# Ten of twelve normalised tiles of the second MoE turned by DMA in 16-bit words in place of TensorE

## The chip, the cores and the metric

The kernel runs on one core of one Trainium2 chip. The metric is the device time of one execution in microseconds; a kernel's figure is the median of several executions. The engines are named as in the profile: PE is TensorE (matmuls and, with an identity matrix as operand, transposes), ACT is ScalarE, DVE is VectorE, POOL is GpSimd, and SP is SyncE, which issues the DMAs here.

## The reference

The program is a chain of three blocks. All results are float32, to float32's accuracy.

```
attn = masked attention: q, k, v of 2 batches x 8 heads x 768 tokens x 64; a key counts for a query when
       the 6 sign bits of q @ proj and k @ proj agree; softmax; times v
x  = attn as 1536 tokens x 512
# first MoE
h  = x @ w_in (512 x 2048);  g = h * tanh(softplus(h));  x = g @ w_out (2048 x 512)
# second MoE
h  = x @ w_in (512 x 1024);  sm = softmax(h);  solu = h * sm
ln = (solu - mean(solu)) / sqrt(var(solu) + 1e-6) * g_ln
out = ln @ w_out (1024 x 512)
```

The change concerns the last line: `ln` comes out of the normalisation with tokens on partitions, and the product with `w_out` wants the 1024 features on partitions, so every tile of 128 tokens x 1024 features has to be turned.

## The kernel before

A matmul in float32 accuracy is made of three matmuls in the shorter type FP32R: each operand is split into a high part (ACT, a copy that rounds) and a low part (DVE or POOL, the difference), and high times high, high times low and low times high are summed in PSUM.

The second MoE goes over the 1536 tokens in 12 tiles of 128. Its steps have these names in the planner and these lines in the profile:

- `sy` (L918 on ACT, L920 on DVE): the split of the tile's 512 input features into high and low.
- `u2` (L927, L928, L931): 24 matmuls of 128x512 into two PSUM banks, the tile's `h`.
- `n2` (L939 to L966): the softmax and the normalisation as a chain of 14 steps between DVE and ACT. Step 0 is the row maximum of `h` (L939, DVE), step 1 the exponential into the SBUF tile `e` (L941, ACT), step 4 `e` times `h` (L947, DVE; the last reader of `h`), step 6 the squares (L952, ACT), steps 7 and 8 the inverse root (L954, L956, ACT), steps 9 to 12 its refinement on 128x1 columns (L958 to L964, DVE), step 13 the normalised tile, again in `e` (L966, DVE).
- `t2` (L974): eight 128x128 float32 transposes on PE into two PSUM banks.
- `l2` (L980 on ACT, L983 on DVE): the high and low part of each half (512 columns) of the turned tile, `lh` and `ll`.
- `d2` (L991, L992, L993): 2 x 12 matmuls of 128x512 with `w_out`.
- `ot` (L997, ACT) copies the result out of PSUM and `od` (L1002) stores it with a DMA from SP's queue.

Each engine has one instruction stream that it works off in order. That order is written by a planner, `program_order` and `Order.run`: every step is an operation with its engine, a cost, a due time and the buffers that it reads and writes; a list-scheduling pass picks, engine by engine, what is ready first, and the instructions are then recorded in exactly that order. Buffers are rings: an operation that opens a new buffer waits until the last reader of the one `n` places before has finished. For the second MoE `h2=2` (two pairs of banks for `h`), `t2=1`, `e2=3` (three tiles `e`), `lh=3` (three pairs `lh`/`ll`), `ot=2`. The numbers are given twice, in the dictionary `rings` for the planner and as `bufs` of the tile pools.

In the attention block some score tiles are already turned by DMA: `tdma` (L1254) issues `dma_start_transpose` from SP on the high and low float16 parts of a tile, 128 x 1536 two-byte values, that is 12 blocks of 128 x 128. That step's input is made by ACT (L1229) and POOL (L1251).

Of the kernel before, what the change touches and what calls it, by code (L numbers as in the profile page):

```python
# [9 lines left out]
F32 = mybir.dt.float32  # L10
F32R = mybir.dt.float32r
F16 = mybir.dt.float16
I32 = mybir.dt.int32
AF = mybir.ActivationFunctionType
ALU = mybir.AluOpType
# [18 lines left out]
    load=19.06, vload=18.96, split0=-188.88, rest0=28.62, split1=-216.02, rest1=37.27, turn=-44.19,  # L34
# [22 lines left out]
    up=0.7, a0=0.494, a1=0.335, a2=0.602, a3=0.613, a4=0.52, a9=0.52, a10=1.25, da=0.464, db=0.2265,  # L57
    sy0=0.52, sy1=0.602, u2=1.39, n0=1.131, n1=1.091, n2=0.069, n3=0.075, n4=1.196, n5=0.069, n6=1.133,
    n7=0.188, n8=0.094, n9=0.069, n10=0.13, n11=0.069, n12=0.069, n13=0.723, t2=0.87, d2=2.72,
)  # L60
WIRE = dict(load=1.3, load0=0.65, vload=1.3, wload=1.65, copy=1.08, bdma=0.2, tdma=1.6,
            od=0.728, const0=0.185, const1=0.028, const2=0.028, const3=0.448)
LATENCY = dict(
    PE=dict(PE=0.0, Activation=0.2, DVE=0.2, Pool=0.2, SP=0.1),
# [10 lines left out]
class Order:  # L75
# [38 lines left out]
    def shared(self, o):  # L114

        key, engine = o[0], o[1]
        if engine == "Pool":
            return True
        if engine != "DVE":
            return False  # L120
        k = key[0]
        if k in ("hi", "sy"):
            return True
        if k == "first":
            return True
        if k == "w":
            return key[2] == 6
        if k == "n2":
            return key[3 - 1] == 13
        return False  # L130
# [5 lines left out]
    def run(self):  # L136
        ops, n = self.ops, len(self.ops)
# [13 lines left out]
        free = dict(BEGIN)  # L151
# [49 lines left out]
        for _ in range(n):  # L201
            best = None
            for e, line in queue.items():
                cand = []
                for r, i in line:
                    r = max(r, free[e])
                    if ops[i][7]:
                        r = ring(i, r)[0]
                        if r is None:
                            continue  # L210
                    cand.append((r, due[i], i))
                if not cand:
                    continue
                first = min(cand)[0]
                pick = min((c for c in cand if c[0] <= first + self.slack), key=lambda c: c[1:])
                if best is None or pick[0] < best[0]:
                    best = (pick[0], e, pick[2])
            at, e, i = best
            o = ops[i]
            queue[e] = [x for x in queue[e] if x[1] != i]  # L220
            for tok, name, m, k in ring(i, at)[1]:
                place[tok] = k
                held[name][k:k + m] = [tok] * m
            for tok in o[7]:
                if tok[0] in taken:
                    taken[tok[0]].append(tok)
            start[i] = at
            if o[8] is not None:
                hw = max(at + 0.05, hw) + o[2]
                begin = max(hw + 0.65, wire)  # L230
                wire = done[i] = begin + o[8]
                if e == "SP":
                    free[e] = begin + 0.85 if o[0][0] == "tdma" else hw
                else:
                    free[e] = at + 0.05
            else:
                if shared[i]:
                    at = start[i] = max(at, port[other[e]])
                    port[e] = at + o[2]
                free[e] = done[i] = at + o[2] * (2 if e == "PE" and at < COLD and o[0][0] != "warm" else 1)  # L240
            got.append(i)
            for tok in o[10]:
                busy[tok] -= 1
                was = idle.setdefault(tok, {})
                was[frm[i]] = max(was.get(frm[i], 0.0), done[i])
            for j in then[i]:
                left[j] -= 1
                if not left[j]:
                    queue[ops[j][1]].append((ready(j), j))
# [17 lines left out]


def program_order(pairs, tiles, routes, evac, chunks, wide, due, rings, stores, slack, queues=(), pooled=0,
                  gates=(0, 0, 0, 0), early=8, attention_only=False, split="G", again="AA", soon=0):  # L270

    order = Order(rings, stores, slack, due)
    op = order.op
    span = 2 * tiles
    lead = -2.0 * span
    A, V, G, T = "Activation", "DVE", "Pool", "PE"
# [255 lines left out]
    for t in range(12):  # L532
        at = N0 + t * TN
        b = 2 - t // 4
        ys = ("yp",) if t == 0 else ("xs", 0, (t - 1) % 4)
        yn = [("yn", b, o) for o in range(4)]
        for g in range(2 if b == 1 else 1):
            n = 2 if b == 1 else 1
            op(("sy", t, g, 0), A, COST["sy0"] / n, at, "sy0", yn, [ys])
            op(("sy", t, g, 1), V, COST["sy1"] / n, at, "sy1", yn, [ys])  # L540
        for kk in range(4):
            behind = [("mi", 47, 2), ("w", 47, 4)] if t == kk == 0 else []
            op(("u2", t, kk), T, COST["u2"], at, "u2", [ys, ("ws", 8 + 2 * kk), ("ws", 9 + 2 * kk)], [("h2", t)], 0,
               behind)
        h, e, s = ("h2", t), ("e2", t), ("s2", t)
        chain = [(V, [h, ("room", 3)], [s]), (A, [h, s], [e, s]), (V, [s], [s]), (V, [s], [s]), (V, [h, s, e], [e, s]),
                 (V, [s], [s]), (A, [e, s], [("j2", t), s]), (A, [s], [s]), (A, [s], [s]), (V, [s], [s]), (V, [s], [s]),
                 (V, [s], [s]), (V, [s], [s]), (V, [e, s], [e])]
        for i, (en, r, w) in enumerate(chain):
            op(("n2", t, i), en, COST["n%d" % i], at, "n%d" % i, r, w)  # L550
        op(("t2", t), T, COST["t2"], at, "t2", [e], [("t2", t)])
        for a in range(2):
            op(("l2", t, a, 0), A, COST["x1"], at, "l0", [("t2", t)], [("lh", t, a)])
            op(("l2", t, a, 1), V, COST["x2"], at, "l1", [("t2", t)], [("lh", t, a)])
        for a in range(2):
            op(("d2", t, a), T, COST["d2"], at, "d2",
               [("lh", t, a)] + [("xs", 2 - a, k) for k in range(4)], [("o2", t)])
        op(("ot", t), A, COST["x1"], at, "ot", [("o2", t)], [("ot", t)])
        dma(("od", t), at, "od", [("ot", t)])
# [19 lines left out]
def lsh_attention_moe_kernel(  # L579
# [17 lines left out]
    ab=2,  # L597
    nb=3,
    gb=2,
    cb=1,  # L600
    lnb=3,
    eb=8,
    p16b=6,
    ptb=8,
# [1 line left out]
    early=5,  # L606
# [3 lines left out]
    gates=(0, 0, 0, 0),  # L610
# [4 lines left out]
    split="G",  # L615
    again="VV",
    soon=4,
):
    nc = tc.nc
    B, H, S, D = q.shape  # L620
# [7 lines left out]
    DF2 = w2_in.shape[1]  # L628
# [62 lines left out]
    pools, parts, raw_w = {}, {}, {}  # L691
# [86 lines left out]
    def two_banks(*tok):  # L778
        return banks[:, order.place[tok]:order.place[tok] + 2]
# [6 lines left out]
    def step(name, make):  # L786

        def run(*key):
            if key[-1] == 0:
                gen[name, key[:-1]] = make(*key[:-1])  # L790
            next(gen[name, key[:-1]])
        return run
# [108 lines left out]
    ysp, ln_t, lt_t, out_t = ({} for _ in range(4))  # L901
# [31 lines left out]
    def norm2(t):  # L933
        h = two_banks("h2", t).rearrange("p a n -> p (a n)")
        s = pools["st2"].tile([128, 16], F32, tag="s", name="s")
        col = lambda i: s[:, i:i + 1]
        e = pools["tm2"].tile([128, DF2], F32, tag="e", name="e", bufs=3)
        ln_t[t] = e
        nc.vector.reduce_max(col(0), h, axis=AX.X, negate=True)  # L939
        yield  # L940
# [9 lines left out]
        yield  # L950
        junk = pools["tm2"].tile([128, DF2], F16, tag="j", name="j", bufs=1)
        nc.scalar.activation(junk, e, AF.Square, bias=col(5), accum_out=col(6))  # L952
# [16 lines left out]
    def turn2(t):  # L969
        e = ln_t.pop(t)  # L970
        tp = two_banks("t2", t).rearrange("p a n -> p (a n)")
        for j in range(NF2):
            js = slice(j * 128, (j + 1) * 128)
            nc.tensor.transpose(tp[:, js], e[:, js], ident)  # L974

    def split2(t, a, part):
        src = two_banks("t2", t)[:, a]
        if part == 0:
            lt_t[t, a] = [pools["ln"].tile([128, 512], F32R, tag=x, name=x) for x in ("lh", "ll")]
            nc.scalar.activation(lt_t[t, a][0], src, AF.Copy)  # L980
        else:
            hi, lo = lt_t[t, a]
            nc.vector.tensor_tensor(lo, src, hi.bitcast(F32), op=ALU.subtract)  # L983
# [340 lines left out]
    for w in v_t:  # L1324
# [3 lines left out]
    due.update(phi)  # L1328
    rings = dict(e=eb, p16=p16b, pt=ptb, vr=2, v=2, r0=rb, r1=rb, sp0=1, sp1=1, A0=hb, A1=hb, B=2 * hb, bb=2 * hb,
                 z=1, wr=wrb, wf=wrb, wr2=wsb, wf2=wsb, am=4, am2=4, pw=4, nr=4, m=8,  # L1330
                 h=2, q=1, wq=1, a=ab, n=nb, c=cb, gh=gb, gl=gb, h2=2, t2=1, o2=2, e2=3, j2=1, s2=4, lh=lnb, ot=2)
    stores = dict(
        bank=(8, dict(warm=1, s=2, st=2, sb=2, sv=1, t=1, o=1, tx=1, h=1, q=1, wq=1, y0=1, y1=1, y2=1, y3=1, h2=2, t2=2, o2=1)),
        store=(ns, dict(e=1, p16=1, pt=1)),
    )
    order = program_order(NP, NC, routes, evac, nconv, is_wide(w1_in), due, rings, stores, slack, queues, pooled, gates,
                          early, split=split, again=again, soon=soon)
    keys = order.run()
    do = dict(
        warm=warm, load=load_qk, load0=load_first, split=qk_split, rest=qk_rest, const=const_in, begin=begin,  # L1340
# [3 lines left out]
        bias=row_bias, exp=exps, hi=hi_part, lo=lo_part, tdma=turn_dma, tr=turn_half, thi=half_high,  # L1344
        tlo=half_low, weigh=weigh, norm=step("norm", norm), open=reopen, wload=w_load, w=step("w", w_steps),
        x=step("x", turn_x), up=up, mi=mish, da=down_high, db=down_low, ky=keep_y,
        sy=split_y, u2=up2, n2=step("n2", norm2), t2=turn2, l2=split2, d2=down2, ot=take, od=put,
    )
    engines = ("PE", "Activation", "DVE", "Pool", "SP")
    with tc.manual_schedule(engines={getattr(mybir.EngineType, e) for e in engines}):  # L1350
# [29 lines left out]
```

## Time and profile before

| | us |
|---|---|
| median of 3 runs | 663.17 |
| lowest, highest of them | 656.47, 664.47 |
| profiled execution, its own time | 663.35 |
| its span in the trace | 661.6 |

| busy, whole span | us | share | instructions |
|---|---|---|---|
| PE | 630.6 | 95% | 4540 |
| DVE | 549.8 | 83% | 1129 |
| ACT | 432.7 | 65% | 702 |
| POOL | 339.1 | 51% | 261 |

The span begins at the first instruction of the program and ends with the last; the 1.75 us between it and the execution's own time lie around it. The page's shares are means over three very different blocks, so the second MoE, which takes the last 140 us, has to be read by windows. There a row of a matmul or a transpose shows how long that instruction was in the pipelined engine; how fast PE works off a run of them is read from the starts.

### The profile page before, as it was taken

The numbers are of one execution on the slowest core, as the hardware profiler recorded it, in microseconds if no ns is written. First come the engines' busy times: TensorE is split into PE (matmuls) and PEld (weight loads), VectorE is DVE, ScalarE is ACT, GpSimd is POOL, SyncE is SP. The second block draws the span as 40 slices with busy tenths as digits, with TensorE's granted clock in tenths as the row PEclk, the third lists the DMA queues.
The fourth block names the chain that finished last, engine by engine and source line by source line (L and its number), as shares of the span: only waits on it lengthen the run. The fifth ranks groups of instructions, "written<-read, shape, count | busy, mean of one in ns | idle before, by whom it ended". The sixth has DMA issues, their size and how long they took to land.

```text
span 661.6 us, 12270 instructions
## 1 busy us (share of the span) xinstructions
PE 630.6 (95%) x4540; PEld 521.3 (79%) x4540; DVE 549.8 (83%) x1129; ACT 432.7 (65%) x702; POOL 339.1 (51%) x261
## 2 busy tenths in 40 slices
PE   7889999899899899999999999999999999999997
PEld 6668788888779788788777777788788888888886
DVE  5889698798989999999999999999999776545440
ACT  5798797899899986756566566655565453525331
POOL 4777868677766576566566765455565200000000
PEclk9999799899999999999999999999999999999999
DMA  7888878989899682222223331111120000000011
GB/s 201 218 184 143 225 165 161 151 182 181 169 194 175 159 196 68 92 64 78 84 95 95 119 104 65 63 64 63 65 92 5 1 0 1 33 16 33 17 49 48
DMA packets 125148, 68.11 MB, mean 103 GB/s; under 512 B 103584, under 2 KB 118048, under 8 KB 125088
## 3 DMA queue, kind: packets, MB, share of 16 engines
q1 hardware_dynamic: 125088, 67.33, 42.5%
q8 instruction: 35, 0.57, 0.4%
q14 instruction: 25, 0.20, 0.1%
HBM read 34.68 MB, written 3.15 MB: 57 GB/s over the span
## 4 chain that ended last, share of the span: by engine, by line
PE 46%; DVE 16%; ACT 5%; issue 4%; DMA 3%; POOL 1%; SPq 0%; DVEq 0%; ACTq 0%; POOLq 0%
PE banks L822 3%; PE banks L824 3%; PE banks L823 3%; PE banks L991 3%; PE banks L931 3%; PE banks L993 3%; PE banks L928 3%; PE banks L927 3%; PE banks L992 3%; PE banks L878 3%; PE banks L883 3%; PE banks L879 3%; DVE a L852 2%; DVE a L840 2%; DVE a L850 2%
## 5 line engine op out<-in xcount | busy, mean ns | idle before, releaser
L1251 POOL TENSOR_TENSOR store<-store 128x768 f16<-128x768 f32 x64 | 104.9, 1652 | 49.9 <-ACT store L1229 37.9
L1218 ACT ACTIVATE store<-banks,mx 128x768 f32<-128x768 f32 x96 | 92.3, 994 | 14.4 <-PE banks L1271 5.2
L1209 DVE TENSOR_REDUCE mx<-banks 128x1 f32<-128x768 f32 x96 | 89.4, 946 | 3.2 <-PE banks L1202 2.2
L856 POOL TENSOR_TENSOR n<-c,a 128x512 f32<-128x512 f32 x48 | 63.8, 1329 | 44.6 <-DVE a L852 42.3
L864 POOL TENSOR_TENSOR gl<-n,gh 128x512 fp32r<-128x512 f32 x48 | 62.9, 1311 | 33.4 <-ACT gh L861 32.9
L822 PE MATMUL banks<-xh,w 128*128 128x512 f32 x192 | 76.6, 399 | 2.5 <-DVE a L852 1.7
L878 PE MATMUL banks<-gh,w 128*128 128x512 f32 x192 | 76.0, 396 | 1.0 <-ACT gh L861 0.8
L824 PE MATMUL banks<-xh,w 128*128 128x512 f32 x192 | 75.7, 394 | 0.0
L823 PE MATMUL banks<-xl,w 128*128 128x512 f32 x192 | 75.5, 393 | 0.0
L879 PE MATMUL banks<-gh,w 128*128 128x512 f32 x192 | 75.4, 393 | 0.0
L883 PE MATMUL banks<-gl,w 128*128 128x512 f32 x192 | 72.7, 396 | 0.0
L846 ACT ACTIVATE a<-n,two 128x512 f32<-128x512 f32 x48 | 34.8, 724 | 57.5 <-DVE n L842 57.3
L730 POOL TENSOR_TENSOR w<-wf,w 128x512 fp32r<-128x512 f32 x40 | 51.7, 1293 | 35.6 <-ACT w L728 35.5
L1202 PE MATMUL banks<-A,A 128*128 128x384 f32 x192 | 57.7, 382 | 8.9 <-ACT store L1218 7.6
L1269 PE MATMUL banks<-v,store 128*128 128x65 f16 x576 | 60.9, 195 | 2.4 <-DVE store L1246 1.9
L1270 PE MATMUL banks<-v,store 128*128 128x64 f16 x576 | 60.8, 196 | 0.0
L1271 PE MATMUL banks<-v,store 128*128 128x65 f16 x576 | 60.5, 193 | 0.0
L1269 PEld LDWEIGHTS <-store 128*128 128x128 f16 x576 | 53.5, 97 | 5.3 <-issue 4.5
L1270 PEld LDWEIGHTS <-store 128*128 128x128 f16 x576 | 53.9, 98 | 3.0 <-issue 2.5
L1271 PEld LDWEIGHTS <-store 128*128 128x128 f16 x576 | 54.0, 99 | 0.0
L1229 ACT ACTIVATE store<-store 128x768 f16<-128x768 f32 x64 | 53.3, 848 | 0.6 <-DMA store<-store 0.3
L1202 PE MATMUL banks<-B 76*128 76x384 f32 x192 | 50.9, 347 | 0.0
(125 smaller groups left out, 1699.3 us busy)
## 6 DMA issues: line engine op xcount, KB each, us to landing
wr<-in_moe_w_in_dram SPq DMA_DIRECT2D x24, 512.0 KB
wr<-in_moe_w_out_dram SPq DMA_DIRECT2D x24, 512.0 KB
vr<-in_v_dram SPq DMA_DIRECT2D x8, 384.0 KB
B<-A SPq DMA_DIRECT2D x16, 192.0 KB
out_dram<-ot SPq DMA_DIRECT2D x12, 256.0 KB
q<-in_q_dram SPq DMA_DIRECT2D x7, 384.0 KB
k<-in_k_dram SPq DMA_DIRECT2D x7, 384.0 KB
B<-bits SPq DMA_DIRECT2D x32, 36.0 KB
```

Of the source, the lines that this page charges most:

```text
L822: nc.tensor.matmul(h, lhsT=wh[:, ks], rhs=xh, start=(kk == 0), stop=False)
L823: nc.tensor.matmul(h, lhsT=wh[:, ks], rhs=xl, start=False, stop=False)
L824: nc.tensor.matmul(h, lhsT=wl[:, ks], rhs=xh, start=False, stop=(kk == KD - 1))
L878: nc.tensor.matmul(y, lhsT=wh[:, os], rhs=g_t[u][0], start=first, stop=False)
L879: nc.tensor.matmul(y, lhsT=wl[:, os], rhs=g_t[u][0], start=False, stop=False)
L883: nc.tensor.matmul(y, lhsT=wh[:, os], rhs=g_t[u][1], start=False, stop=last)
L1202: nc.tensor.matmul(s[:, half, 0:NH], lhsT=opnd[nm, p, j, 0][:, cc], rhs=opnd[nm, p, j, 1][:, hs], start=(i == 0), stop=(i == 1),)
L1218: nc.scalar.activation(kept("e", t).rearrange("p (a n) -> p a n", a=2), two_banks("s", t)[:, :, 0:NH], AF.Exp, bias=m[:, 3:4], scale=m[:, ...
L1251: nc.gpsimd.tensor_tensor(p16[:, 1], kept("e", t), p16[:, 0], op=ALU.subtract)
L1269: nc.tensor.matmul(o, lhsT=pt[:, 0, kc, :], rhs=vh, start=(kc == 0), stop=False)
L1270: nc.tensor.matmul(o[:, 0:D], lhsT=pt[:, 0, kc, :], rhs=vl, start=False, stop=False)
L1271: nc.tensor.matmul(o, lhsT=pt[:, 1, kc, :], rhs=vh, start=False, stop=(kc == NC - 1))
```

## The change

For tiles 0 to 9 (`by_dma=10`) the eight transposes `t2` are gone. In their place each half (512 columns, `a`) of `e` goes through these steps, for the upper (`x=0`) and lower (`x=1`) 16-bit words of its float32 values:

- `wd`: the words, which lie at every second 16-bit place, are copied into a dense tile `wd` of 128x512 uint16; the upper ones by ACT, the lower ones by POOL.
- `td`: a `dma_start_transpose` from SP's queue turns the four 128x128 blocks of `wd` into the tile `wt`.
- `mg`: `wt` is copied back into the every-second-word places of the same half of `e`; the upper words by DVE, the lower ones by POOL.

`l2` then reads `e` in SBUF where it read PSUM. Tiles 10 and 11 are turned on PE as before. The ring of `e` goes from three to two, and that of `lh`/`ll` from three to two; `wd` and `wt` get two buffers for each word. The planner has costs for the new steps, and it treats `mg` as it treats other operations that share a port between DVE and POOL.

```diff
@@ COST, WIRE, Order.shared, Order.run
+    wd0=0.5, wd1=0.65, mg0=0.6, mg1=0.65,
-WIRE = dict(load=1.3, ..., tdma=1.6,
+WIRE = dict(load=1.3, ..., tdma=1.6, td=0.55,
-        if k in ("hi", "sy"):
+        if k in ("hi", "sy", "mg"):
-                    free[e] = begin + 0.85 if o[0][0] == "tdma" else hw
+                    free[e] = begin + 0.85 if o[0][0] in ("tdma", "td") else hw
@@ program_order
-        op(("t2", t), T, COST["t2"], at, "t2", [e], [("t2", t)])
+        if t >= by_dma:
+            op(("t2", t), T, COST["t2"], at, "t2", [e], [("t2", t)])
         for a in range(2):
-            op(("l2", t, a, 0), A, COST["x1"], at, "l0", [("t2", t)], [("lh", t, a)])
-            op(("l2", t, a, 1), V, COST["x2"], at, "l1", [("t2", t)], [("lh", t, a)])
+            src = ("t2", t)
+            if t < by_dma:
+                src = ("mg", t, a)
+                for x in range(2):
+                    op(("wd", t, a, x), (A, G)[x], COST["wd%d" % x], at, "wd", [e], [("wd%d" % x, t, a)])
+                    dma(("td", t, a, x), at, "td", [("wd%d" % x, t, a)], [("wt%d" % x, t, a)])
+                for x in range(2):
+                    op(("mg", t, a, x), (V, G)[x], COST["mg%d" % x], at, "mg", [("wt%d" % x, t, a), e], [src])
+            src = [src, e] if t < by_dma else [src]
+            op(("l2", t, a, 0), A, COST["x1"], at, "l0", src, [("lh", t, a)])
+            op(("l2", t, a, 1), V, COST["x2"], at, "l1", src, [("lh", t, a)])
@@ lsh_attention_moe_kernel
-    lnb=3,
+    lnb=2,
+    by_dma=10,
-        e = pools["tm2"].tile([128, DF2], F32, tag="e", name="e", bufs=3)
+        e = pools["tm2"].tile([128, DF2], F32, tag="e", name="e")
+    def word(x):
+        return x.bitcast(U16).rearrange("p (n w) -> p n w", w=2)
+    def words_out(t, a, x):
+        w = wd_t[t, a, x] = pools["tm2"].tile([128, 512], U16, tag="wd%d" % x, name="wd")
+        src = word(ln_t[t][:, a * 512:(a + 1) * 512])[:, :, 1 - x]
+        if x:
+            nc.gpsimd.tensor_copy(w, src)
+        else:
+            nc.scalar.activation(w, src, AF.Copy)
+    def words_turn(t, a, x):
+        w = wt_t[t, a, x] = pools["tm2"].tile([128, 4, 128], U16, tag="wt%d" % x, name="wt")
+        nc.sync.dma_start_transpose(out=w, in_=wd_t.pop((t, a, x)))
+    def words_in(t, a, x):
+        dst = word(ln_t[t][:, a * 512:(a + 1) * 512])[:, :, 1 - x]
+        src = wt_t.pop((t, a, x)).rearrange("p c n -> p (c n)")
+        (nc.gpsimd if x else nc.vector).tensor_copy(dst, src)
     def split2(t, a, part):
-        src = two_banks("t2", t)[:, a]
+        src = ln_t[t][:, a * 512:(a + 1) * 512] if t < by_dma else two_banks("t2", t)[:, a]
-    ... h2=2, t2=1, o2=2, e2=3, j2=1, s2=4, lh=lnb, ot=2)
+    ... h2=2, t2=1, o2=2, e2=2, j2=1, s2=4, lh=lnb, ot=2, wd0=2, wd1=2, wt0=2, wt1=2, mg=2)
```

The planner's order is the same up to the first `u2` steps and another one behind them. In the changed kernel the lines are larger by 13 in `n2` (L952 is the maximum, L960 `e` times `h`, L965 the squares, L979 the last step of the normalisation) and by 36 behind it; `wd` is L1001 on ACT and L999 on POOL, `td` L1005, `mg` L1010, `l2` L1016 and L1019, `ot` L1033, `od` L1038.

PE's stream, in steps: before, behind the start-up, it holds `d2`, the next tile's `t2`, and now and then two `u2` in a row; the changed one alternates strictly, u2 of tile 6, d2 of tile 3, u2 of tile 7, d2 of tile 4, and so on to u2 of tile 11, d2 of tile 8, the first half of d2 of tile 9, t2 of tile 10, the second half of d2 of tile 9, d2 of tile 10, t2 of tile 11, d2 of tile 11.

**DVE, at the maximum of tile 6.** Before, it is followed by the split of an input tile, three `ll` of tiles 0 and 2, and the steps 2 to 5 of tile 5:

```order
L939 TENSOR_REDUCE s<-banks 128x1
L920 TENSOR_TENSOR ys<-yn,ys 128x512
L983 TENSOR_TENSOR ll<-banks,lh 128x512 x3
L943 TENSOR_SCALAR s<-s 128x1
L945 RECIPROCAL s<-s 128x1
L947 SCALAR_TENSOR_TENSOR e,s<-e,s,banks 128x1024
L949 TENSOR_SCALAR s<-s 128x1
```

Now the `ll` there is that of tile 3's second half, and the upper words of tile 4's first half (`mg`) come in between:

```order
L952 TENSOR_REDUCE s<-banks 128x1
L933 TENSOR_TENSOR ys<-yn,ys 128x512
L1019 TENSOR_TENSOR ll<-e,lh 128x512
L1010 COPY e<-wt 128x512
L956 TENSOR_SCALAR s<-s 128x1
L958 RECIPROCAL s<-s 128x1
L960 SCALAR_TENSOR_TENSOR e,s<-e,s,banks 128x1024
L962 TENSOR_SCALAR s<-s 128x1
```

With `e` in a ring of two, step 1 of tile 5 (ACT) opens the buffer that this `ll` reads last.

**ACT, at the end of the program.** Before, the high parts of tile 11 (the last `lh` pair) stand ahead of the `ot` of tile 10, and PE has all of `d2` of tile 10 between t2 of tile 11 and its use:

```order
L956 ACTIVATE s<-s 128x1
L997 ACTIVATE ot<-banks 128x512
L980 ACTIVATE lh<-banks 128x512 x2
L997 ACTIVATE ot<-banks 128x512
L980 ACTIVATE lh<-banks 128x512 x2
L997 ACTIVATE ot<-banks 128x512
L980 ACTIVATE lh<-banks 128x512 x2
L997 ACTIVATE ot<-banks 128x512 x2
```

Now the normalisation of tile 11 (L965 to L969) stands behind the `lh` of tile 10, and the `lh` of tile 11 behind the `ot` of tile 10:

```order
L1016 ACTIVATE lh<-banks 128x512
L965 ACTIVATE j,s<-e,s 128x1024
L967 ACTIVATE s<-s,eps 128x1
L969 ACTIVATE s<-s 128x1
L1033 ACTIVATE ot<-banks 128x512
L1016 ACTIVATE lh<-banks 128x512 x2
L1033 ACTIVATE ot<-banks 128x512
```

**SP's queue, from tile 3's store to tile 6's.** Before, this queue holds only the stores `od` here. Now four transposes of a tile stand between two stores:

```order
L1038 DMA out_dram<-ot 128x512
L1005 DMA_TRANSPOSE wt<-wd 128x4x128 x4
L1038 DMA out_dram<-ot 128x512
L1005 DMA_TRANSPOSE wt<-wd 128x4x128 x4
L1038 DMA out_dram<-ot 128x512
L1005 DMA_TRANSPOSE wt<-wd 128x4x128 x4
```

## Rows read from the trace of the kernel before

**Rows 1.** Windows of the second MoE: busy us (x instructions) by engine.

```profile
core 0: us, PE busy (x) PEld busy (x) DVE busy (x) ACT busy (x) POOL busy (x), PEclk, DMA share, GB/s
523.00:540.00 17.00, 17.00 (x85) 14.19 (x84) 12.31 (x26) 8.39 (x18) 0.00 (x0) 1.00 0.01 1
...
sum 134.00, PE 134.00 PEld 111.81 DVE 70.42 ACT 54.20 POOL 0.00; mean PE 19.14 PEld 15.97 DVE 10.06 ACT 7.74 POOL 0.00
```

**Rows 2.** Chain of waits, 620 to 662 us: start, duration, what.

```profile
639.77 0.87 PE banks L974 x8
646.11 0.87 PE banks L974 x8
```

**Rows 3.** PE in order of time at tile 11's transposes: start, duration, line, operands.

```profile
645.71 0.39 PE L993 MATMUL banks<-w,ll 128*128 128x512 f32 x1
645.95 1.03 PE L974 MATMUL banks<-cs,e 128*128 128x128 f32 x8
646.74 0.48 PE L991 MATMUL banks<-w,lh 128*128 128x512 f32 x1
647.05 0.40 PE L992 MATMUL banks<-w,lh 128*128 128x512 f32 x1
647.28 0.39 PE L993 MATMUL banks<-w,ll 128*128 128x512 f32 x1
```

**Rows 4.** ACT in order of time, tile 11 (bracket: idle before, and what ended it).

```profile
628.12 1.12 ACT L941 ACTIVATE e<-banks,s 128x1024 f32<-128x1024 f32 x1
631.33 1.15 ACT L952 ACTIVATE j<-e,s 128x1024 f16<-128x1024 f32 x1 [0.20 <-DVE s L949]
...
646.64 0.59 ACT L980 ACTIVATE lh<-banks 128x512 fp32r<-128x512 f32 x1
```

**Rows 5.** DVE in order of time, the same tile.

```profile
631.02 0.08 DVE L947 DVE_READ_ACCUMULATOR e<-e,s,banks 128x1 f32 x1
633.80 0.81 DVE L966 TENSOR_SCALAR e<-e,s 128x1024 f32<-128x1024 f32 x1
647.26 0.69 DVE L983 TENSOR_TENSOR ll<-banks,lh 128x512 fp32r<-128x512 f32 x1 [2.75 <-ACT lh L980]
```

**Rows 6.** DVE at the start of the stage, where POOL still works.

```profile
512.73 1.22 DVE L939 TENSOR_REDUCE s<-banks 128x1 f32<-128x1024 f32 x1
514.46 1.10 DVE L920 TENSOR_TENSOR ys<-yn,ys 128x256 fp32r<-128x256 f32 x1
516.32 0.42 DVE L920 TENSOR_TENSOR ys<-yn,ys 128x256 fp32r<-128x256 f32 x1
```

**Rows 7.** POOL beside it.

```profile
513.99 1.30 POOL L864 TENSOR_TENSOR gl<-n,gh 128x512 fp32r<-128x512 f32 x1 [2.24 <-ACT gh L861]
517.41 1.29 POOL L856 TENSOR_TENSOR n<-c,a 128x512 f32<-128x512 f32 x1 [2.13 <-DVE s L943]
```

**Rows 8.** Groups by line: count, busy us, mean ns, idle before.

```profile
L1101 POOL TENSOR_SCALAR sp<-q 128x768 fp32r<-128x768 f32 x7 | 5.8, 830 | 9.7 <-DMA q<-in_q_dram 9.0 <-PE banks L1127 0.7
L730 POOL TENSOR_TENSOR w<-wf,w 128x512 fp32r<-128x512 f32 x40 | 51.7, 1293 | 35.6 <-ACT w L728 35.5
L918 ACT ACTIVATE ys<-yn 128x512 fp32r<-128x512 f32 x4 | 2.5, 624 | 6.5 <-PE banks L928 6.5
```

**Rows 9.** Line L1254, issues of the attention's transposes: ns min/median/max.

```profile
L1254 SPq DMA_TRANSPOSE store<-store x64: 1284/1435/2580, 24.6 to 244.4; - x64
```

**Rows 10.** SP, then PE, in order of time; DMA engines' busy tenths, 244:249, 40 slices.

```profile
244.36 1.52 SPq L1254 DMA_TRANSPOSE store<-store  x1
249.13 0.20 PE L1269 MATMUL banks<-v,store 128*128 128x65 f16 x1
DMA  9920000000003999999999991000000000024249
```

**Rows 11.** DMA issues in 100:200.

```profile
store<-store SPq DMA_TRANSPOSE x28
```

**Rows 12.** Waits, 540 to 662 us: total, times, longest.

```profile
ACT lh L980 <- PE banks L992: 22.8, 10, 8.3
```

More of the change, by code (lines that the diff above doesn't have):

```diff
@@ L12 @@
 F16 = mybir.dt.float16
+U16 = mybir.dt.uint16
 I32 = mybir.dt.int32
@@ L59 @@
     n7=0.188, n8=0.094, n9=0.069, n10=0.13, n11=0.069, n12=0.069, n13=0.723, t2=0.87, d2=2.72,
+    wd0=0.5, wd1=0.65, mg0=0.6, mg1=0.65,
 )
-WIRE = dict(load=1.3, load0=0.65, vload=1.3, wload=1.65, copy=1.08, bdma=0.2, tdma=1.6,
+WIRE = dict(load=1.3, load0=0.65, vload=1.3, wload=1.65, copy=1.08, bdma=0.2, tdma=1.6, td=0.55,
             od=0.728, const0=0.185, const1=0.028, const2=0.028, const3=0.448)
@@ L269, in program_order @@
 def program_order(pairs, tiles, routes, evac, chunks, wide, due, rings, stores, slack, queues=(), pooled=0,
-                  gates=(0, 0, 0, 0), early=8, attention_only=False, split="G", again="AA", soon=0):
+                  gates=(0, 0, 0, 0), early=8, attention_only=False, split="G", again="AA", soon=0, by_dma=0):
     order = Order(rings, stores, slack, due)
@@ L974, in turn2 @@
             nc.tensor.transpose(tp[:, js], e[:, js], ident)
+    def word(x):
+        return x.bitcast(U16).rearrange("p (n w) -> p n w", w=2)
+    wd_t, wt_t = {}, {}
+    def words_out(t, a, x):
[12 more added lines that the diff above has]
+        (nc.gpsimd if x else nc.vector).tensor_copy(dst, src)
     def split2(t, a, part):
-        src = two_banks("t2", t)[:, a]
+        src = ln_t[t][:, a * 512:(a + 1) * 512] if t < by_dma else two_banks("t2", t)[:, a]
         if part == 0:
@@ L1330, in lsh_attention_moe_kernel @@
                  z=1, wr=wrb, wf=wrb, wr2=wsb, wf2=wsb, am=4, am2=4, pw=4, nr=4, m=8,
-                 h=2, q=1, wq=1, a=ab, n=nb, c=cb, gh=gb, gl=gb, h2=2, t2=1, o2=2, e2=3, j2=1, s2=4, lh=lnb, ot=2)
+                 h=2, q=1, wq=1, a=ab, n=nb, c=cb, gh=gb, gl=gb, h2=2, t2=1, o2=2, e2=2, j2=1, s2=4, lh=lnb, ot=2, wd0=2, wd1=2, wt0=2, wt1=2, mg=2)
     stores = dict(
@@ L1336, in lsh_attention_moe_kernel @@
     order = program_order(NP, NC, routes, evac, nconv, is_wide(w1_in), due, rings, stores, slack, queues, pooled, gates,
-                          early, split=split, again=again, soon=soon)
+                          early, split=split, again=again, soon=soon, by_dma=by_dma)
     keys = order.run()
@@ L1346, in lsh_attention_moe_kernel @@
         x=step("x", turn_x), up=up, mi=mish, da=down_high, db=down_low, ky=keep_y,
-        sy=split_y, u2=up2, n2=step("n2", norm2), t2=turn2, l2=split2, d2=down2, ot=take, od=put,
+        sy=split_y, u2=up2, n2=step("n2", norm2), t2=turn2, wd=words_out, td=words_turn, mg=words_in, l2=split2, d2=down2, ot=take, od=put,
     )
```

## The prediction

> **What bounds the kernel now.** I read the windows of the last stage first. From 523 to 657 us PE is busy for all 134 us, its granted clock is 1.00, the upper of its two levels (2.4 GHz), POOL does nothing and DVE and ACT are busy for half of the time [rows 1]. The waits agree: ACT and DVE wait for PE, ACT's `lh` for 22.8 us in all [rows 12]. So in this stage every microsecond that leaves PE leaves the end time, provided that nothing else becomes late. The reader should then look at how PE's instructions start, since a row's own duration includes the pipeline: matmul starts are 0.23 us apart [rows 3].
>
> **What is removed.** Across one tile's eight transposes the starts of `L993` and of the second matmul behind them are 647.05 - 645.71 = 1.34 us apart; without transposes these are two steps of 0.23, so a tile's transposes cost 1.34 - 0.46 = 0.88 us of PE [rows 3]. Ten tiles: **-8.8 us**, all of it on the path. That is also the most the change can give: nothing else is taken from PE, and its 24 matmuls of a `u2` or `d2` stay at 6.34 (two tiles' transposes, 639.77 to 646.11, apart [rows 2]) - 0.88 = 5.46 us. One tile's `u2` and `d2` thus take 10.9 us, the beat of the changed stage.
>
> **What is added off PE.** Per tile: on ACT two copies `wd`, on POOL two `wd` and two `mg`, on DVE two `mg`, on SP four issues. ACT's copy of 128x512 from SBUF takes 0.62 us [rows 8]. For POOL no row shows a 16-bit copy: its one-input operation takes 0.83 us for 768 elements, 0.55 for 512, its two-input one 1.29 for 512 [rows 8]; those are my bounds and I take 0.6, since a copy has one input. DVE's copy I bound by 0.42 (a 256-wide operation alone, [rows 6]) and 0.82 (the 1024-wide one-input operation, [rows 5]). Sums per beat of 10.9 us: ACT +1.2, POOL 2.4 (5.2 at most), DVE +0.8 to 1.6. At half-empty engines this costs nothing by itself. `l2` reads SBUF where it read PSUM; I leave it at its rows' 0.6 and 0.7.
>
> SP: an issue takes 1.43 us for a transpose of twelve blocks, 2.58 at the highest [rows 9]. The new one has four blocks; I bound it by 0.5 (a third) and 1.43 and reckon with 1.43. Four are 5.7 us of a beat, and the store `od` between them goes to memory that nobody waits for; even four at 2.58 would fit. The DMA engines: the last transpose of the attention is issued at 244.36, the engines are idle until 245.5 (slice 12 of 0.125 us) and busy until 247.1; its first reader starts at 249.13 [rows 10]. So twelve blocks need 1.15 us to begin and 1.6 us of transfer; four would be done 1.7 us after the issue (1.15 + 0.53). From issue to use I bound by 1.7 and 4.8 (249.13 - 244.36) and take 2.2, near the lower end, because the row is an end-to-end one with three times the data and its reader had other work first.
>
> **Where it could become late, and the loop that decides.** ACT's and DVE's streams are in order, and `l2` of a tile stands ahead of the squares of the next one. So the way from one tile's last normalisation step to the next tile's is a loop, once per beat: `wd` and hand-over 0.8, SP's first issue 1.43, second issue to landing 2.2, POOL's `mg` 0.6, `lh` 0.6 [rows 4], the squares to the end of step 13 of the next tile 633.80 + 0.81 - 631.33 = 3.3 [rows 4, 5], hand-overs 0.4 (0.20 each, [rows 4]). Together **9.3 us**, against a beat of 10.9: it fits, with 1.6 us to spare. With the lower values it is 7.9, with the upper ones (4.8 landing, 1.29 POOL) 12.6. The ring of `e` at two asks that step 1 of a tile waits for `ll` two tiles before; from there to that point is under two beats when the loop fits.
>
> **What is lost on the way in.** Before, PE ran several `u2` ahead. Now it alternates, and around tiles 3 to 6 the planned order has little slack. Take u2 of tile 7, which needs tile 5's banks. From the end of u2 of tile 6: the maximum 1.22 [rows 6], the input split and the `ll` of tile 3 at 0.69 each [rows 5], step 1 to the end of step 4 of tile 5, 631.10 - 628.12 = 2.98 [rows 4, 5], two hand-overs 0.4: 6.0 us, while PE has d2 of tile 3, 5.46, to do. PE waits 0.5 us. The `mg` in this piece runs under ACT's exponential. Four places are of this kind by the order (second halves of d2 of tiles 1 and 3, u2 of tiles 6 and 7): at 0.5 each **+2.0 us**, between 0 and 4.
>
> On DVE and POOL: the same 128x256 operation with two SBUF inputs takes 0.42 us with POOL idle and 1.10 us started at 514.46, while POOL's 513.99 operation runs until 515.29 [rows 6, 7]. DVE's new `mg`, its `ll` (now two SBUF inputs) and step 13 can therefore wait for a POOL copy, which I put into the upper end of the 0 to 4. The Trainium skill, SBUF - State Buffer, "Who interferes with whom", says that such a pair is locked for the whole of the instruction that came first; by it a DVE operation waits at most one POOL copy, and the trace agrees (1.10 - 0.42 = 0.68 of the 1.30).
>
> **At the end.** d2 of tile 11 now follows directly on t2 of tile 11. In the rows ACT starts `lh` 0.69 us behind the first transpose and needs 0.59; with 0.2 hand-over PE could go on at 647.43 where it went on at 646.74: 0.7 us. `ll` ends at 647.95, so the third matmul waits another 0.3 [rows 3, 4, 5]. **+1.0 us** (0.7 to 1.5). What follows, `ot` and the last store, is unchanged.
>
> **Sum.** Against the profiled execution, 663.35 us (span 661.6): 663.35 - 8.8 + 2.0 + 1.0 = 657.5. The median of the runs is 663.17, 0.2 less; I predict **657.5**, 0.9% faster, a third of what would count as more than no change (2%, 13 us, is about what a measurement of this kernel can tell).
>
> **Rivals.**
>
> 1. *Everything is hidden* but the end's minimum: 663.35 - 8.8 + 0.7 = 655. For it: waits of PE inside the stage were zero before. Against: the 6.0 against 5.46. Chance 0.14.
> 2. *The hand-overs are dearer*, through the port of DVE and POOL or a copy near its upper bound: 4 + 1.5 in place of 3 gives 660, with a loop just over the beat up to 663. Chance 0.16.
> 3. *Slower than before: the loop is longer than the beat.* Place: the lower words' way wd, td, mg over POOL and SP, ahead of the squares on ACT. It binds from 10.9 us. From there each tile costs the excess, eight times (tiles 2 to 9). The gain of 5.8 is gone at 10.9 + 5.8 / 8 = 11.6, that is 2.3 us more than I take, say a landing of 4.5 us. At the upper values, 12.6, it costs 1.7 x 8 = 13.6: 671. For it: two issues and a landing per half are serial, and a small DMA has the same start as a large one. Against: rows 10 bound the landing well below for three times the data. Chance 0.12.
> 4. *The DMA engines' rate binds.* Sixteen blocks a tile at the measured 1.6 / 12 = 0.13 us are 2.1 us of a beat; 28 transposes of 12 blocks in 100 us [rows 11] bound it by 0.30 a block, 4.8 us a tile. To bind, a block would need 0.68 us; at twice that, 10.9 us more for each of ten tiles, about 766. Chance 0.01. The Trainium skill, VectorE: DVE Perf Modes, "The three transpose paths" and "Rules for kernel authors", speaks against this change: it gives 1309 ns for a 128x128 block by DMA against 390 ns by TensorE, and advises TensorE where a PSUM result will do. By that figure a tile would take 20.9 us and the kernel about 757 us; the trace does not agree, since its blocks take 0.30 us or less.
>
> The forecast has 0.57. That PE waits but the transposes were no load at all, I exclude: the 1.34 us are starts of PE's own stream.
>
> **Range and chances.** The runs of the kernel before lie between 656.5 and 664.5, so that a median can sit some 3 us off. Low end: rival 1, 655, less 3 of scatter, 652. High end: rival 2 and the beginning of rival 3, 666. Faster by over 2% (below 650) lies outside the sum: 0.02. Slower by over 2% (above 676.5) asks for a loop of 13.3 us, over all bounds, or rival 4: 0.04. Within 2%: 0.94.
>
> **What would show it.** Right: PE without `L974` but for 16 instructions; POOL with 40 copies from 523 us on, near 0.6 us; u2 and d2 alternating without gaps from tile 8 on, waits of PE under 1 us around u2 of tiles 6 and 7, and about 1 us between the last transposes and the last d2; a stage shorter by 5 to 6 us. Wrong: waits of PE for DVE's `ll` or `e` in every beat (rival 3), POOL copies above 1.3 us, issues of SP that wait for each other's landing, or a first MoE that changed, which I take to be the same since its orders are.

## The result and the profile after

| | before | after |
|---|---|---|
| median, us | 660.85 (9 executions) | 654.92 (9 executions) |
| lowest, highest | 656.47, 667.29 | 651.61, 656.66 |
| profiled execution, its span | 663.35, 661.6 | 653.04, 651.3 |
| stage: first u2 matmul to the start of the last matmul | 150.40 | 143.22 |

The ratio of the two is 0.9885, with an interval from 0.9855 to 0.9915: 5.6 to 9.6 us faster. The interval leaves out 1, and the gain is under 2%; single executions of the two kernels still meet at the ends (656.47 before, 656.66 after). The forecast was 657.5.

The profiled executions differ by 10.3 us, which is more than the change did. The stage is the part to compare, since the two orders agree up to the first u2. These are its first and last matmul; the columns are start, duration, line and operands. Before the change:

```profile
507.09 0.39 PE L927 MATMUL banks<-w,ys 128*128 128x512 f32 x1
...
657.49 0.39 PE L993 MATMUL banks<-w,ll 128*128 128x512 f32 x1
```

and after it:

```profile
504.01 0.39 PE L940 MATMUL banks<-w,ys 128*128 128x512 f32 x1
...
647.23 0.39 PE L1029 MATMUL banks<-w,ll 128*128 128x512 f32 x1
```

657.49 - 507.09 = 150.40 and 647.23 - 504.01 = 143.22: the stage gives **7.18 us**. The other 3.1 us were already there when it began (507.09 against 504.01), in instructions whose order the change leaves alone; the section on the hardware returns to them.

In the windows of the stage after the change (busy us and instructions by engine, as in [rows 1]) PE is short of full by 0.10 and 0.06 us in two windows and then full until 640. POOL, idle before, is busy for 4 to 6 us of each 20 until 620:

```profile
540.00:560.00 20.00, 19.90 (x87) 16.07 (x86) 12.87 (x29) 11.47 (x23) 4.13 (x6) 1.00 0.28 66
560.00:580.00 20.00, 19.94 (x88) 16.13 (x87) 12.75 (x30) 11.86 (x24) 5.82 (x8) 1.00 0.28 73
580.00:600.00 20.00, 20.00 (x90) 16.45 (x88) 13.49 (x31) 10.50 (x21) 5.32 (x8) 1.00 0.28 73
```

Busy time hides short gaps, so the starts have to be read. The first row here is the last matmul of d2 of tile 3, the next the first one of u2 of tile 7; they start 0.45 us apart where 0.23 is the usual step, and the next two 0.34:

```profile
573.21 0.39 PE L1029 MATMUL banks<-w,ll 128*128 128x512 f32 x1
573.66 0.50 PE L940 MATMUL banks<-w,ys 128*128 128x512 f32 x1
574.00 0.39 PE L941 MATMUL banks<-w,ys 128*128 128x512 f32 x1
```

The same in DVE's rows, the chain that this u2 waited for, from the maximum of tile 6 to the end of step 4 of tile 5 (L960):

```profile
568.17 1.23 DVE L952 TENSOR_REDUCE s<-banks 128x1 f32<-128x1024 f32 x1 [1.73 <-PE banks L944]
569.31 0.68 DVE L933 TENSOR_TENSOR ys<-yn,ys 128x512 fp32r<-128x512 f32 x1
569.91 0.69 DVE L1019 TENSOR_TENSOR ll<-e,lh 128x512 fp32r<-128x512 f32 x1
570.51 0.46 DVE L1010 COPY e<-wt 128x512 uint16<-128x512 uint16 x1
...
572.32 1.28 DVE L960 SCALAR_TENSOR_TENSOR e<-e,s,banks 128x1024 f32<-128x1024 f32 x1
```

There is one other gap in the stage proper, 0.25 us ahead of the third matmul of d2 of tile 2, which needs DVE's `ll`:

```profile
556.87 0.39 PE L1028 MATMUL banks<-w,lh 128*128 128x512 f32 x1
557.35 0.50 PE L1029 MATMUL banks<-w,ll 128*128 128x512 f32 x1
```

That `ll` (556.62 to 557.30) stands on DVE behind a copy `mg` and an input split that ran beside one of POOL's new copies and took 1.12 us where the row at 569.31 has 0.68, that is 0.44 more than usual and more than the gap (a row of DVE, then one of POOL):

```profile
555.58 1.12 DVE L933 TENSOR_TENSOR ys<-yn,ys 128x512 fp32r<-128x512 f32 x1
555.25 0.90 POOL L999 COPY wd<-e 128x512 uint16<-128x512 uint16 x1
```

At the end, PE's rows around the transposes of tile 11 answer to [rows 3]:

```profile
640.28 1.03 PE L987 MATMUL banks<-cs,e 128*128 128x128 f32 x8
641.61 0.50 PE L1027 MATMUL banks<-w,lh 128*128 128x512 f32 x1 [0.30 <-ACT lh L1016]
641.95 0.40 PE L1028 MATMUL banks<-w,lh 128*128 128x512 f32 x1
642.34 0.50 PE L1029 MATMUL banks<-w,ll 128*128 128x512 f32 x1
642.67 0.39 PE L1027 MATMUL banks<-w,lh 128*128 128x512 f32 x1
```

From the first transpose to the fourth matmul behind them it is 642.67 - 640.28 = 2.39 us; before, it was 647.51 - 645.95 = 1.56 (the first three starts in [rows 3]). The end costs 0.83 us: 0.54 ahead of the first matmul and 0.29 in the three steps that follow.

The new instructions, by line (count, busy us, mean ns, idle before and its reason), 520 to 652 us:

```profile
L1010 POOL COPY e<-wt 128x512 uint16<-128x512 uint16 x20 | 16.0, 799 | 48.4 <-DMA wt<-wd 48.4
L999 POOL COPY wd<-e 128x512 uint16<-128x512 uint16 x20 | 12.6, 654 | 32.1 <-DVE e L979 32.1
L1001 ACT ACTIVATE wd<-e 128x512 uint16<-128x512 uint16 x20 | 11.6, 623 | 14.3 <-DVE e L979 14.3
L1010 DVE COPY e<-wt 128x512 uint16<-128x512 uint16 x20 | 9.6, 480 | 1.9 <-DMA wt<-wd 1.9
```

POOL waits 48.4 us for the DMAs, and that costs next to nothing: ACT's `lh` waited for POOL 0.2 us in the whole stage. What counts of an idle engine is who waits for it.

### The profile page after: what moved, and what is told of

It reads as the page before. It is cut to its first block, busy times and chain, and to the rows that moved or that the text cites. A ratio compares the mean times of both kernels' runs of the same rounds, so it can differ in the third digit from the quotient of the medians.

```text
span 651.3 us, 12308 instructions
## 1 busy us (share of the span) xinstructions
PE 622.2 (96%) x4460; PEld 513.1 (79%) x4460; DVE 558.7 (86%) x1149; ACT 444.0 (68%) x722; POOL 367.5 (56%) x301
## 4 chain that ended last, share of the span: by engine, by line
PE 42%; DVE 22%; ACT 6%; issue 5%; DMA 1%; POOL 0%; DVEq 0%; ACTq 0%; SPq 0%
PE banks L835 4%; PE banks L837 3%; PE banks L940 3%; PE banks L836 3%; PE banks L944 3%; PE banks L941 3%; PE banks L896 3%; PE banks L891 3%; PE banks L892 3%; PE banks L1029 3%; PE banks L1027 3%; DVE mx L1245 3%; PE banks L1028 3%; DVE a L865 2%; DVE a L853 2%
## 5 line engine op out<-in xcount | busy, mean ns | idle before, releaser
L1254 ACT ACTIVATE store<-banks,mx 128x768 f32<-128x768 f32 x96 | 92.4, 998 | 12.3 <-DVE mx L1250 5.0
L1305 PE MATMUL banks<-v,store 128*128 128x65 f16 x576 | 60.0, 193 | 2.3 <-DVE store L1282 1.9
L1307 PE MATMUL banks<-v,store 128*128 128x65 f16 x576 | 59.6, 192 | 0.0
L1305 PEld LDWEIGHTS <-store 128*128 128x128 f16 x576 | 53.0, 96 | 5.0 <-issue 4.6
L1306 PEld LDWEIGHTS <-store 128*128 128x128 f16 x576 | 53.3, 97 | 2.9 <-issue 2.5
L1307 PEld LDWEIGHTS <-store 128*128 128x128 f16 x576 | 53.5, 99 | 0.0
```

The source lines that it names most:

```text
L1254: nc.scalar.activation(kept("e", t).rearrange("p (a n) -> p a n", a=2), two_banks("s", t)[:, :, 0:NH], AF.Exp, bias=m[:, 3:4], scale=m[:, ...
L1305: nc.tensor.matmul(o, lhsT=pt[:, 0, kc, :], rhs=vh, start=(kc == 0), stop=False)
L1306: nc.tensor.matmul(o[:, 0:D], lhsT=pt[:, 0, kc, :], rhs=vl, start=False, stop=False)
L1307: nc.tensor.matmul(o, lhsT=pt[:, 1, kc, :], rhs=vh, start=False, stop=(kc == NC - 1))
```

## The experiments

All stages are from one profiled execution of each kernel.

**The transposes back on PE.** Everything of the change stays; PE does eight transposes whose result nobody reads ahead of the first half of d2 of tiles 0 to 9.

```diff
         o = bank("o2", t)
         hi, lo = lt_t.pop((t, a))
+        for j in range(8 if a == 0 and t < by_dma else 0):
+            nc.tensor.transpose(o[:, (j % 4) * 128:(j % 4 + 1) * 128], ident, ident)
```

> The change with eight 128x128 transposes of a constant put back into PE's stream ahead of each of the ten d2, their result unread; every engine's order is otherwise the change's. I measure the stage from the first u2 matmul to the start of the last matmul: 150.4 us before, 143.2 in the change. Theory (the gain is PE time, 0.88 us a tile, less 1.4 us of new PE waits): 151.0 to 152.0, that is about 1 us longer than before, and the kernel's time the same as before within its scatter. Rival (the gain comes from something else that the change does: other order, DMA, a shorter chain off PE): the stage stays near 143 to 146 and the time about 7 us below before.

Measured: stage 151.23, median 662.32, ratio to before 1.0014 (0.9986 to 1.0041). 8.0 us came back, and with them before's time. It is 8.0 and not 8.8 because the transposes give DVE time in the two places where the change waits: both gaps are gone. The wait at the end is still there, and the stage is just its 0.83 us longer than before. With PE's time put back nothing of the gain is left.

**No turn at all.** `wd`, `td` and `mg` are left out; `l2` reads `e` as it came out of the normalisation, so the product is taken of unturned data.

```diff
     def words_out(t, a, x):
+        return
     def words_turn(t, a, x):
+        return
     def words_in(t, a, x):
+        return
```

> The change without wd, td and mg at all: e of tiles 0 to 9 goes into l2 as it is, not turned, so the output is not the reference's; the remaining order is the change's. Theory (all that was added off PE is hidden but for 0.7 us of PE waits between tiles 1 and 7): 142.4 to 143.2 us, at most 0.8 shorter than the change. Rival (copies, transposes or the shared port cost the change several us): 140 to 141.5.

Measured: stage 142.81, median 654.50, ratio 0.9904 (0.9870 to 0.9939). 80 operations on three engines and 40 DMAs cost 0.4 us together. The wait at u2 of tile 7 (0.22 us, ahead of 574.40) and those at the end (steps of 0.57, 0.34, 0.39 and 0.34 us, as in the change) remain without them: these belong to the new order, not to the turn. The gap for `ll` is gone: that one is the turn's, and it makes up nearly all of the 0.4.

**Rings of two alone.**

```diff
-    by_dma=10,
+    by_dma=0,
```

> All twelve tiles turned by PE, but with the change's rings of two for e and for lh/ll, in the order that the planner makes of that. Theory (the rings alone neither gain nor cost): 150.0 to 151.5 us, time as before. Rival (rings of two make PE wait, and the change's gain is net of that): 152 to 158.

Measured: stage 150.31, median 661.48, ratio 0.9994 (0.9964 to 1.0025). One tile `e` and one pair `lh`/`ll` less cost nothing in that order.

**The loop, made longer.** POOL's copy back into `e` made five times, then three and two times, in the change's order.

```diff
-        (nc.gpsimd if x else nc.vector).tensor_copy(dst, src)
+        for _ in range(5 if x else 1):
+            (nc.gpsimd if x else nc.vector).tensor_copy(dst, src)
```

> The change with POOL's copy back (mg, lower words) made five times over in place of once, 4 x 0.55 to 0.8 us more at that place, 40 copies become 120 in all on POOL; order unchanged. Theory (the loop wd, td, mg, lh, squares, step 13 binds when it is longer than the beat of 10.9 us; measured parts of the change's loop add up to 9.8): loop 12.0 to 13.0, 1.1 to 2.1 us over the beat for eight tiles less 2.1 us of lead: stage 7 to 15 us longer than the change, 150 to 158. Rival (POOL costs only when it is busy all the time; its work is then 7 to 9 us of a beat): no more than 1 us longer, 143 to 144.5.

Measured: stage 170.86, 27.6 us over the change; median 681.63, ratio 1.0307 (1.0265 to 1.0350). The direction is the theory's, the size nearly twice its upper end. The steps 13 (L979) of successive tiles stood 13.67 us apart, three times in a row, so something closed there; I took it for the loop of the prediction, concluded from 13.67 - 4 x 0.82 that the change's loop is 10.4 us, and put that to the test with three and two copies.

> The change, with each of POOL's 20 copies back into e (mg) made three times, order as it is. Stage: first u2 matmul to the start of the last matmul, 143.2 us in the change. With five copies the steps 13 of neighbouring tiles stood 13.67 us apart three times in a row, against 10.9 us of TensorE's matmuls for a tile, and the stage was 27.6 us longer: some ten tiles of 2.77 us. Theory: the loop through the halves' turn binds there, with one half's group of copies in it, so two copies less are 2 x 0.82 us less: 12.0 us, 1.1 us over TensorE's, and ten tiles of it make the stage 154 us (151 to 157). Rival, the prediction's own loop of 9.3 us: with two copies more it is 11.0, equal to TensorE's tile: 143 to 145.5. Second rival, the 27.6 us were the price of TensorE's lower clock behind its waits and not of the loop: about half of 27.6 for half of the copies, with no steady distance between the steps 13.

Measured: stage 146.73, 3.5 us over the change. My corrected theory (154) fell, and so did the third (157). The prediction's loop had said 11.0 us; the steps 13 stand 11.12, 11.09 and 11.07 us apart. Its stage forecast, at most 145.5, was passed by 1.2 us. Of the 3.5 us, 1.3 stand on the way in, at the third matmul of d2 of tile 2, where the change waits 0.25 us and this kernel 1.52; 2.0 stand in front of starts from 597 us on, where the loop closes. The chain of waits between two steps 13 in this kernel shows the loop itself, in order of time (start, duration, what):

```profile
611.53 0.82 DVE e L979
612.38 1.15 ACT wd L1001 x2
613.53 0.53 ACT lh L1017
...
614.32 2.36 DMA wt<-wd
...
616.83 0.77 POOL e L1011
...
617.65 0.78 POOL e L1011
...
618.47 0.78 POOL e L1011
619.27 0.64 ACT lh L1017
619.94 0.74 DVE ll L1020
620.68 0.94 DVE e L1011
...
622.62 0.82 DVE e L979
```

One round is 622.62 - 611.53 = 11.09 us. Each copy takes 0.82 with its hand-over; an estimate for the round without the two extra ones is 11.09 - 1.64 = **9.45 us**, against the prediction's 9.3. This is DVE in the kernel with five copies, around the same step:

```profile
640.05 1.03 DVE L1011 COPY e<-wt 128x512 uint16<-128x512 uint16 x1
641.89 0.59 DVE L977 TENSOR_TENSOR s<-s 128x1 f32<-128x1 f32 x1
642.51 1.39 DVE L979 TENSOR_SCALAR e<-e,s 128x1024 f32<-128x1024 f32 x1
```

and in the one with three:

```profile
633.50 0.16 DVE L977 TENSOR_TENSOR s<-s 128x1 f32<-128x1 f32 x1
633.70 0.81 DVE L979 TENSOR_SCALAR e<-e,s 128x1024 f32<-128x1024 f32 x1
```

With five, POOL's ten copies of a tile run without a break from 634.70 to 643.3, over DVE's last steps: L977 takes 0.59 in place of 0.16, L979 1.39 in place of 0.81, together 1.0 us more in the loop. 9.45 + 4 x 0.82 + 1.0 = 13.7: that is the 13.67. My 10.4 had put DVE's delay into the loop of the change, where POOL is quiet at that point.

> The same with POOL's copies made twice. Theory, loop of 10.4 us in the change: 11.2 us, 0.3 us over TensorE's tile: stage 144 to 147.5 us, against 143.2. Prediction's loop of 9.3 us: 10.1, under it: 143 to 144. A cost that grows by the copy, whatever bounds the loop (27.6 us for four, 6.9 for each): 150.

Measured: stage 143.87, within the 143 to 144 of the prediction's loop and just under the range of the theory with 10.4. Two copies cost 0.65 us and five 27.6: a threshold, not a price by the copy. The 0.65 stand at one place, the third matmul of d2 of tile 2: it waits 0.25 us with one copy, 0.90 with two and 1.52 with three. Only there, on the way in, does each copy have its price before the loop closes. The medians of these two kernels (654.73 and 654.84, four executions each, ratios 0.9899 and 0.9894) are the change's own; for three copies that does not match a stage 3.5 us longer, for which the last section has a likely reason, TensorE's clock in the attention block.

**Other numbers of tiles.**

```diff
-    by_dma=10,
+    by_dma=5,      # and, as a kernel of its own, 11
```

> The change for five tiles in place of ten. Theory, the gain is the tiles' own transposes, 0.88 us each, and the waits on the way in stay at under 1 us: stage 143.2 + 4.4 = 147.6 (147 to 148.5). Rival, the gain comes from the rings, the moved instructions or the way into the stage and not by the tile: the change's 143 to 144.5. Second rival, the way out of the turned tiles costs as the way in does: 148.5 to 150.

Measured: stage 146.83, median 659.14, ratio 0.9967 (0.9934 to 0.9999). It is 0.2 under the lower end of my range, because I had counted from the change's stage, whose 0.83 us at the end five tiles do not have: PE's starts show no gap there. With five, 5 x 0.88 less 0.77 of waits on the way in gives 3.6, measured 3.57; with ten, 8.8 less 0.67 and 0.83 gives 7.3, measured 7.18. That both come to 0.71 to 0.72 a tile is luck.

> The change for eleven tiles in place of ten; the planner then sets five halves of d2 behind the last u2, then the transposes of tile 11, then the last three halves. Theory (TensorE's transposes are saved as long as the turn has time): tile 10's first half is called for some 633.9 us on the change's clock, and by the row of five copies the way from step 13 to lh takes 1.42 + 4.44 + 0.79 + 0.54 = 7.2 us behind 628.8: 636.0, so TensorE waits about 2.1 us there, and about 1 us more for tile 11's step 13; less 0.88 for the eight transposes and 0.5 for the waits before the last tile that now have cover: stage 144 to 146.5, no faster than with ten. Rival, each tile is worth its transposes wherever it stands: 142.3.

Measured: stage 146.62, just over the range; median 658.02, ratio 0.9961 (0.9924 to 0.9998). The eleventh tile costs 3.4 us in place of giving 0.9. PE in order of time, at the first half of d2 of tile 10 (from 639.15):

```profile
636.41 0.40 PE L1029 MATMUL banks<-w,ll 128*128 128x512 f32 x1
639.15 0.50 PE L1027 MATMUL banks<-w,lh 128*128 128x512 f32 x1 [2.34 <-ACT lh L1016]
639.48 0.43 PE L1028 MATMUL banks<-w,lh 128*128 128x512 f32 x1
639.88 0.80 PE L1029 MATMUL banks<-w,ll 128*128 128x512 f32 x1
640.47 0.63 PE L1027 MATMUL banks<-w,lh 128*128 128x512 f32 x1
640.89 0.63 PE L1028 MATMUL banks<-w,lh 128*128 128x512 f32 x1
```

and the windows of it:

```profile
636.00:640.00 4.00, 1.66 (x7) 0.75 (x5) 2.72 (x8) 2.64 (x6) 0.77 (x1) 0.96 0.47 131
640.00:644.00 4.00, 4.00 (x13) 3.15 (x14) 2.35 (x4) 0.63 (x1) 0.76 (x1) 0.61 0.02 4
644.00:650.00 6.00, 6.00 (x32) 5.07 (x31) 1.39 (x2) 1.68 (x3) 0.00 (x0) 1.00 0.11 44
```

The wait is the expected one (2.5 us for 2.1); the further 1 us expected at tile 11's transposes is not there. What I had not reckoned with is behind the wait: matmuls start 0.42 us apart in place of 0.23, and the granted clock of 640 to 644 is 0.61. The ten steps from 639.15 to 643.31 take 4.16 us, 1.9 more than at 0.23. Ten tiles are the better number of these three.

## Why the prediction was right, and where its sizes were off

- **-8.8 for the transposes on PE: right.** Putting them back brings the stage back to 151.23.
- **Beat and loop: right, the size in part by luck.** 10.9 against 9.3 was the question of the slower rival. In the change the loop does not close; 9.45 is the estimate from where it does, with three copies. Its terms there: four issues of SP in 5.16 us, 1.3 each (taken: 1.43); 2.4 us of transfer and 0.15 to POOL's start behind it (2.2); 0.82 for POOL's copy (0.6); 3.5 from `ll` to the end of step 13 (3.3 from the squares on). Smaller and larger errors cancelled. The last piece also runs another way than the prediction had it: the chain goes over DVE's `ll` and `mg`, not over ACT's squares and roots; the two ways end together in that round, at 621.62 and 621.60. The slack is borne out, since one more copy fits and two do not.
- **The added work off PE at nothing: right**, 0.4 us by the kernel without the turn, nearly all of it the gap for `ll`.
- **+2.0 on the way in: the term that was mis-sized.** Of "four places, at 0.5 each" one shows a gap, u2 of tile 7: 0.22 us, and 0.1 in the start that follows. The other gap, 0.25 and 0.1, stands where the prediction had none, in the first half of d2 of tile 2; together 0.67. At u2 of tile 7 I had summed durations to 6.0 us; from the start of the maximum to PE's matmul it is 573.66 - 568.17 = 5.49, as DVE's operations start 0.60 apart where each is 0.69 long. PE waits all the same because the maximum starts 0.2 us behind d2's first matmul (567.97), which the sum had left out. By the rows the gap at tile 2 has two sources on DVE, each larger than itself: a copy `mg` (0.35 us from its start at 555.23 to the split's) and the split's 0.44 us beside POOL, the port that the prediction had kept for the upper end of its 0 to 4. They were not tried apart. The three other places have no gap.
- **+1.0 at the end: 0.83**, inside the 0.7 to 1.5 that the text gave.
- **Sum of the stage:** -8.8 + 0.67 + 0.83 = -7.3, measured -7.2, predicted -5.8. The 0.1 between are not assigned to any row.
- **Rivals.** -7.2 lies between the first (everything hidden but 0.7 at the end, -8.1) and the forecast (-5.8), nearer to the first: 0.9 and 1.4 away. The mechanism is the forecast's, PE's time less new waits inside the stage and at its end, with its way in a third as dear. The dearer hand-overs show only as single rows: besides the split above, POOL's copy takes 1.07 where DVE's copy runs beside it and 0.77 alone, and step 13 of tile 3 takes 1.35 where 0.81 is usual. The longer loop needs two copies more. The DMA's rate does not bind: tiles follow each other every 10.9 us with the DMA engines busy for 0.28 to 0.33 of the time. The Trainium skill, VectorE: DVE Perf Modes, "The three transpose paths", has 1309 ns for a block of 128x128; an estimate from that figure, one block behind the other, is 20.9 us for a tile, and the trace does not agree.

The median fell by about what the stage did (5.9 between the medians, 7.6 by the ratio's middle). It is luck that 5.9 is so near the forecast's 5.8, as the stage gave 7.2. It is luck, too, that the median of 654.92 is rival 1's 655: both forecasts were counted down from an execution of 663.35, which lies 2.5 above the median of the nine. The 10.3 us between the profiled executions hold 2.75 from the attention block and 0.3 from the first MoE, whose order the change leaves alone.

## What to carry to other kernels

In a stage where one engine is busy all the time, count work taken from it at its start-to-start time (here 8.8 us) and subtract the waits that the new order makes (1.5). Work put on half-empty engines cost 0.4 us here, because the loop through them was shorter than the bound engine's beat: sum such a loop, engine by engine, and leave a reserve. Sum it from starts, not durations. At the end of this program nothing covers the loop, and the eleventh tile showed what that costs: the last tiles keep the short way.

## What the runs showed of the hardware

**Some waits of PE cost more than their length.** In the kernel with five copies PE waited 3.7 us, and then:

```profile
607.20 0.79 PE L1028 MATMUL banks<-w,lh 128*128 128x512 f32 x1 [3.66 <-ACT lh L1017]
607.79 0.63 PE L1029 MATMUL banks<-w,lh 128*128 128x512 f32 x1
608.25 0.79 PE L1030 MATMUL banks<-w,ll 128*128 128x512 f32 x1
```

```profile
606.00:610.00 4.00, 2.81 (x6) 1.96 (x7) 2.80 (x4) 1.83 (x3) 3.81 (x6) 0.60 0.29 66
```

The first fence is PE in order of time, the second the window around it: the granted clock is 0.60 on the mean, and the matmuls start 0.46 to 0.59 us apart, about twice the 0.23 of the upper level, as the lower one (1.2 GHz) would have it. 2.5 us of waiting with eleven tiles had the same behind it. Shorter waits did not: after 2.0 us ahead of 536.20 with five copies, after 1.5 ahead of 558.74 with three, and after the change's 0.2 to 0.3 the clock stayed at 1.00.

**The scatter between executions goes in part with this clock.** Over the 42 executions of the kernel before that ran beside the experiments the mean is 664.9 us where the mean granted clock of the execution was 0.974 to 0.982 (5 of them), 661.1 at 0.990 to 0.992 (20) and 659.8 at 0.994 to 0.997 (12); the other 5, at 0.986 to 0.989, have 662.8. It is not all: the 20 at 0.990 to 0.992 still spread from 659.2 to 663.6, and the two profiled executions of before and after, both at 0.990, are 2.75 us apart in the attention block. There the clock falls early: from 20 to 40 and 40 to 60 us the profile of the kernel with five tiles shows 0.67 and 0.72 and reaches the first matmul of the first MoE at 234.17 us; that with two copies shows 0.83 and 1.00 and reaches it at 230.90. All ten profiles, in the same order of instructions, lie between 229.07 and 234.89. At 0.990 to 0.992 the change's six executions have a mean of 654.7, 6.4 under before. That fits the kernel with three copies having the change's median: three of its four executions had 0.995 or more, mean 654.4, where the change's only execution at 0.995 took 651.61; one execution does not show it. What decides the clock there was not tried.

**DVE and POOL hold each other up even on 128x1.** L977 on 128x1 went from 0.16 to 0.59 us beside POOL's copies of 0.77, L979 from 0.81 to 1.39 and DVE's copy L1011 from 0.46 to 1.03; with one copy, the input split went from 0.68 to 1.12 beside a copy of 0.90. The Trainium skill, SBUF - State Buffer, "Who interferes with whom", has the pair locked until the first instruction is done; the delays here, 0.43 to 0.58 us, stay under one such copy, which agrees.
